# A fused linear-attention and GELU-MLP block: twelve small DMAs moved to ScalarE's queue, and one scaling step moved between two sums

## The chip, the cores and the metric

The kernel runs on one core of one Trainium2 chip. The metric is the device time of one execution in microseconds (us). Three runs of the kernel before gave 207.22, 206.78 and 206.72 us, a median of 206.78 us.

## What is computed

One input x of 2048 tokens by 640 features is normalised once. The result feeds an attention without softmax (32 heads of 20 features) and a two-layer MLP with 1536 hidden features. Both outputs are added to x. All inputs are bf16.

```python
q, k, v = qkv[0], qkv[1], qkv[2]
phi = lambda t: jnp.where(t > 0, t + 1, jnp.exp(t)) + 1e-6
pq, pk = phi(q), phi(k)
kv = jnp.einsum("bhsd,bhse->bhde", pk, v)
z = jnp.einsum("bhsd->bhd", pk)
num = jnp.einsum("bhqd,bhde->bhqe", pq, kv)
den = jnp.einsum("bhqd,bhd->bhq", pq, z)[..., None] + 1e-6
o = num / den
...
return x + _A_ref(xn, A_wqkv, A_wo) + _B_ref(xn, B_w1, B_b1, B_w2, B_b2)
```

The division by `den` is one number for each token and head. The kernel does it on the query side: it multiplies `pq` by 1/den ahead of the last matrix product.

## The kernel before, in words

**Tiles.** The 2048 tokens are 16 tiles of 128, in four chunks of 512 (`NC` = 4, `CW` = 512). The 640 features are five blocks of 128 (`DT` = 5), the 1536 hidden features twelve (`JT` = 12).

**Stages.** Up to about 127 us the kernel normalises x, computes the hidden activations `HG`, the keys, the key-value products, folds these and `wo` into one matrix `Msb`, and computes the transformed queries `PQ` of all chunks (`q_chunk`). The last stage, from 127 us on, is a single long product: for each output block, twelve matmuls of `W2` with `HG` and five of `Msb` with `PQ` are summed in one PSUM bank. For chunks 0, 1 and 2, and for the last feature block of chunk 3, this is done feature-major by `fm` (line 745). For the rest of chunk 3 it is done token by token in `out_piece` (line 710). For chunks 0 to 2 all five twelve-matmul parts of a chunk come first, and then for each block the five `PQ` matmuls and `fm_out`.

**After a sum.** `fm_out(c, nb)` adds bias and residual on VectorE (line 751), and issues a DMA transpose from SyncE's queue (line 755), which brings the block back to token-major. `fm_store(c)` (line 760, SyncE's queue) stores a chunk once its transposes have landed. `x_turn` and `x_turn_last` (lines 674 and 679) are DMA transposes of the residual, also in SyncE's queue.

**Denominators.** Each chunk passes through six steps before its `PQ` may be used in the product:

- `den_parts(c)`: five VectorE instructions (lines 630 and 633) form the products of `PQ` and z.
- `den_gather(c)`: four DMAs of 64 KB (line 644) bring the four partition groups of a head beside each other.
- `den_inv(c)`: a VectorE sum (line 649) and a reciprocal (line 652).
- `den_spread(c)`: four DMAs of 32 KB (line 658) copy the reciprocals to all partitions of a head.
- `rden_scale(c)`: five VectorE multiplications (line 664) scale `PQ` in place. `PQ` block j of the chunk may enter the product after the j-th.

The buffers of these steps (`yv`, `y4`, `rdv`) lie in the tensor that the profile calls `xn_tm`. So a gather is `xn_tm<-xn_tm` and a spread is `xn_tm<-rden`.

**What sets the order.** Each engine executes its instructions in the order in which the Python code records them. A small planner (`Planner.ins`) adds the semaphore waits. There are no due times. VectorE, TensorE, SyncE and ScalarE each have one queue, and an instruction that waits holds up all those recorded after it on the same engine. SyncE's queue, in order, holds from chunk 1 on: half of gather 1, `x_turn(1)`, half of spread 1, the five transposes of `fm_out(0)`, half of gather 2, half of spread 2, the store of chunk 0, `x_turn(2)`, `x_turn_last`, the five transposes of `fm_out(1)`, half of gather 3, half of spread 3, the store of chunk 1, the five transposes of `fm_out(2)`, the store of chunk 2, the last transpose, and the last stores. ScalarE's queue holds the other halves of the gathers and spreads, and no other work after 128.3 us.

PSUM has eight banks, handed out in turn by `take`.

Of the kernel before, what the change touches and what calls it, by code (L numbers as in the profile page):

```python
# [112 lines left out]
def bass_parallel_sum__linear_attn_block__dense_activation_gelu__prompt_kernel(  # L113
# [24 lines left out]
    with contextlib.ExitStack() as es:  # L138
# [59 lines left out]
        def take(n):  # L198
            b = ring[0]
            if n == 2 and b % 2:  # L200
                b += 1
            b %= 8
            ring[0] = (b + n) % 8
            return b

        def bank(b, lo=0, hi=512):
            return ps[:, b * 512 + lo: b * 512 + hi]
# [427 lines left out]
                       reads=[r_z, r_PQ[c][j], r_y[c % 2]], writes=[r_y[c % 2]])  # L635

        def dma_q(c, q):
            return "scalar" if c and q % 2 else "sync"

        def den_gather(c):  # L640
            for q in range(MH):
                dst = y4[c % 2][H * q:H * (q + 1)]
                src = yv[c % 2][:, SW * q:SW * (q + 1)]
                Pl.ins(dma_q(c, q), lambda e, dst=dst, src=src: e.dma_start(dst, src),
                       reads=[r_y[c % 2]], writes=[r_y4[c % 2][q]], dma=True)

        def den_inv(c):
            s = c % 2
            Pl.ins(v, lambda e: e.tensor_reduce(out=den_sb[:, s, :], in_=y4[c % 2].rearrange("p m s -> p s m"),  # L649
                                                axis=mybir.AxisListType.X, op=ALU.add),  # L650
                   reads=r_y4[c % 2], writes=[r_den[s]])
            Pl.ins(v, lambda e: e.reciprocal(rden[:, s, :], den_sb[:, s, :]), reads=[r_den[s]], writes=[r_rden[s]])

        def den_spread(c):
            for q in range(MH):
                dst = rdv[c][:, SW * q:SW * (q + 1)]
                src = rden[H * q:H * (q + 1), c % 2, :].unsqueeze(1).to_broadcast([H, MH, SW])
                Pl.ins(dma_q(c, q), lambda e, dst=dst, src=src: e.dma_start(dst, src),
                       reads=[r_rden[c % 2]], writes=[r_rdb[c][q]], dma=True)

        def rden_scale(c):
            cc = slice(c * CW, (c + 1) * CW)
            for j in range(DT):
                Pl.ins(v, lambda e, j=j: e.tensor_tensor(out=PQ[:, j, cc], in0=PQ[:, j, cc], in1=rdv[c], op=ALU.mult),  # L664
                       reads=r_rdb[c] + [r_PQ[c][j]], writes=[r_PQ[c][j]])
# [6 lines left out]
        def x_turn(c):  # L672
            for t in range(c * CH, (c + 1) * CH):
                Pl.ins("sync", lambda e, t=t: e.dma_start_transpose(xnT[:, :, t * P:(t + 1) * P], x_res[:, t, :]),  # L674
                       reads=[r_xr[c]], writes=[r_xT[t], r_xnT[t]], dma=True)

        def x_turn_last():
            for t in range(NT - CH, NT):
                Pl.ins("sync", lambda e, t=t: e.dma_start_transpose(xnT[:, DT - 1:DT, t * P:(t + 1) * P], x_res[:, t, CW:D]),  # L679
                       reads=[r_xr[NC - 1]], writes=[r_xT[t], r_xnT[t]], dma=True)  # L680
# [51 lines left out]
        def den_parts(c, lo, hi):  # L732
            for j in range(lo, hi):
                den_part(c, j)

        NF = NC - 1

        def fm(c, nb, b, lo, hi):
            cc = slice(c * CW, (c + 1) * CW)
            ns = slice(nb * P, (nb + 1) * P)  # L740
            for i in range(lo, hi):
                l, r = (W2[:, i, ns], HG[:, i, cc]) if i < JT else (Msb[:, i - JT, ns], PQ[:, i - JT, cc])
                rd = ([r_W2] + [r_HG[t][i] for t in range(c * CH, (c + 1) * CH)] if i < JT
                      else [r_M[nb], r_PQ[c][i - JT]])
                Pl.ins("tensor", lambda e, l=l, r=r, i=i: e.matmul(bank(b), l, r, start=(i == 0), stop=(i == JT + DT - 1)),  # L745
                       reads=rd, writes=[B_[b]], mark=(i == hi - 1))

        def fm_out(c, nb, b):
            o = (c % 2) * DT + nb
            cc = slice(c * CW, (c + 1) * CW)  # L750
            Pl.ins(v, lambda e: e.scalar_tensor_tensor(out=oT[o], in0=bank(b), scalar=b2c[:, nb:nb + 1],  # L751
                                                       in1=xnT[:, nb, cc], op0=ALU.add, op1=ALU.add),
                   reads=[B_[b], r_b2c] + r_xT[c * CH:(c + 1) * CH],
                   writes=[r_oT[o]] + (r_GT + [r_KVT] + [r for m in r_MT for r in m] if c == 0 else []))
            Pl.ins("sync", lambda e: e.dma_start_transpose(x_res[:, c * CH:(c + 1) * CH, nb * P:(nb + 1) * P], oT[o]),  # L755
                   reads=[r_oT[o]], writes=[r_omn[c][nb]], dma=True)

        def fm_store(c, lo=0):
            dst = ov[c * CW:(c + 1) * CW, lo:D].rearrange("(t p) d -> p t d", p=P)
            stores.append(Pl.ins("sync", lambda e: e.dma_start(dst, x_res[:, c * CH:(c + 1) * CH, lo:D]),  # L760
                                 reads=r_omn[c], dma=True))
# [7 lines left out]
        for c in range(NF):  # L769
            bs = [take(1) for nb in range(DT)]  # L770
            for nb in range(DT):
                fm(c, nb, bs[nb], 0, JT)
            for nb in range(DT):
                fm(c, nb, bs[nb], JT, JT + DT)
                fm_out(c, nb, bs[nb])
            if c + 2 < NC:
                den_parts(c + 2, 0, DT)
                den_gather(c + 2)
            rden_scale(c + 1)
            if c + 2 < NC:  # L780
                den_inv(c + 2)
                den_spread(c + 2)
            fm_store(c)
            if c == 0:
                x_turn(2)
                x_turn_last()
# [46 lines left out]
```

## Time and profile before

| | us |
|---|---|
| median of three runs | 206.78 |
| lowest and highest | 206.72, 207.22 |
| the profiled execution | 206.52 |
| its span, first to last instruction | 204.7 |
| outside the span (206.52 less 204.7) | 1.8 |
| TensorE busy (matmul) | 200.3 |
| VectorE busy | 122.4 |
| ScalarE busy | 73.6 |
| GpSimd busy | 14.4 |

The granted TensorE clock was 1.000 over the whole span. Busy times are those of one profiled execution. PE is TensorE's matmul, PEld its weight load, DVE is VectorE, ACT is ScalarE. SPq and ACTq are the queues from which SyncE and ScalarE issue DMAs; the time of such a row is that of the issue, not of the transfer. "To landing" is the time from the start of the issue to the arrival of the data. In the timeline, rows that follow each other on one engine are merged, and "x5" is the number of instructions in a row.

### The profile page before, as it was taken

How to read it: one execution, taken by the hardware profiler on the slowest of the kernel's cores; microseconds unless marked ns; L12 is line 12 of the kernel's file. 1: busy time of each engine (PE TensorE's matmuls, PEld its weight loads, DVE VectorE, ACT ScalarE, POOL GpSimd, SP SyncE). 2: the span in 40 equal slices, each digit the busy share in tenths (PEclk: the TensorE clock that was granted, in tenths of full speed). 3: DMA queues.
4: the chain of work that ended last, by engine and by line, in shares of the span. 5: the costliest groups of instructions: out<-in, count | busy, mean ns of one | idle time of the engine just before them, and what ended most of it. 6: DMA issues, size and time to landing. Idle time of an engine off the chain costs nothing.

```text
span 204.7 us, 3181 instructions
## 1 busy us (share of the span) xinstructions
PE 200.3 (98%) x1170; PEld 106.5 (52%) x1170; DVE 122.4 (60%) x246; ACT 73.6 (36%) x144; POOL 14.4 (7%) x43
## 2 busy tenths in 40 slices
PE   7999999999999999999999999999999999997996
PEld 2799884444444444644456565444444444442444
DVE  4679664000007899999278899596983593068123
ACT  3589886666676555112144695000000000000000
POOL 3145434000000000000000000000000000000000
DMA  5966989799901111000389544115551743407553
GB/s 183 349 241 123 131 169 124 214 325 245 327 6 29 26 26 26 3 0 0 64 245 327 105 96 91 29 26 115 115 126 32 205 90 76 94 25 209 75 160 122
DMA packets 52549, 25.45 MB, mean 124 GB/s; under 512 B 38118, under 2 KB 52534, under 8 KB 52534
## 3 DMA queue, kind: packets, MB, share of 16 engines
q1 hardware_dynamic: 50510, 24.39, 49.3%
q10 hardware_dynamic: 2024, 0.86, 1.6%
q8 instruction: 9, 0.15, 0.3%
q14 instruction: 6, 0.05, 0.1%
HBM read 12.72 MB, written 2.62 MB: 75 GB/s over the span
## 4 chain that ended last, share of the span: by engine, by line
PE 83%; SPq 9%; DMA 3%; DVE 2%; issue 1%; ACT 0%; DVEq 0%; ACTq 0%
PE ps L381 24%; PE ps L745 17%; PE ps L584 11%; PE ps L573 8%; PE ps L532 8%; PE ps L710 7%; SPq L755 3%; SPq L674 3%; SPq L679 2%; PE ps L563 2%; PE ps L523 2%; PE ps L413 1%; DMA xPK<-in_A_x_dram 1%; DMA xn_tm<-rden 1%; DMA xn_tm<-xn_tm 1%
## 5 line engine op out<-in xcount | busy, mean ns | idle before, releaser
L381 PE MATMUL ps<-xnT,W 128*128 128x256 bf16 (+2 forms) x375 | 50.4, 297 | 0.0
L385 ACT ACTIVATE HG<-ps,b1c 128x256 bf16<-128x256 f32 (+2 forms) x75 | 37.4, 522 | 13.2 <-PE ps L381 11.3
L745 PE MATMUL ps<-HG,W 128*128 128x512 bf16 x192 | 42.1, 379 | 0.0
L381 PEld LDWEIGHTS ps<-xnT,W 128*128 128x128 bf16 x375 | 32.4, 98 | 17.4
L745 PEld LDWEIGHTS ps<-HG,W 128*128 128x128 bf16 x192 | 18.8, 98 | 22.6
L584 PE MATMUL ps<-xnT,Wqkv 128*128 128x512 bf16 x100 | 22.8, 379 | 0.0
L745 PE MATMUL ps<-PQ,Msb 128*128 128x512 bf16 x80 | 18.4, 380 | 1.1 <-DVE PQ L664 1.1
L532 PE MATMUL ps<-Wqkv,xnT 128*128 128x512 bf16 x80 | 17.9, 379 | 0.0
L573 PE MATMUL ps<-xPK,xn_tm 128*128 128x512 bf16 x80 | 17.4, 379 | 0.0
L337 DVE BATCH_NORM_STATS2 stats<-xPK 128x6 f32<-128x320 bf16 x32 | 13.7, 470 | 5.6 <-DMA xPK<-in_A_x_dram 5.6
L584 PEld LDWEIGHTS ps<-xnT,Wqkv 128*128 128x128 bf16 x100 | 11.3, 118 | 8.7
L507 ACT ACTIVATE xn_tm<-ps 128x512 bf16<-128x512 f32 x20 | 11.9, 597 | 9.5 <-PE ps L584 8.9
L510 DVE SCALAR_TENSOR_TENSOR PQ<-ps,xn_tm 128x512 bf16<-128x512 f32 x20 | 13.8, 692 | 2.1
L507 ACT ACTIVATE ek<-ps 128x512 bf16<-128x512 f32 x20 | 11.8, 597 | 8.4 <-PE ps L532 6.4
L649 DVE TENSOR_REDUCE den_sb<-xn_tm 128x128 f32<-128x512 f32 x4 | 4.1, 1037 | 17.7 <-DMA xn_tm<-xn_tm 17.7
L518 DVE CAST b2c<-out_l 128x5 f32<-128x5 bf16 x1 | 0.2, 172 | 23.4 <-DMA out_l<-b2bc 23.4
L751 DVE SCALAR_TENSOR_TENSOR W<-ps,b2c,xnT 128x512 bf16<-128x512 f32 x16 | 11.5, 737 | 4.3 <-PE ps L745 3.9
L745 PEld LDWEIGHTS ps<-PQ,Msb 128*128 128x128 bf16 x80 | 7.8, 98 | 11.4 <-DVE PQ L664 2.5
L532 PEld LDWEIGHTS ps<-Wqkv,xnT 128*128 128x128 bf16 x80 | 7.8, 98 | 9.4
L573 PEld LDWEIGHTS ps<-xPK,xn_tm 128*128 128x128 bf16 x80 | 7.8, 98 | 9.3
L633 DVE SCALAR_TENSOR_TENSOR xn_tm<-PQ,z_sb,xn_tm 128x512 f32<-128x512 bf16 x16 | 12.0, 750 | 0.4
L510 DVE SCALAR_TENSOR_TENSOR xPK<-ps,ek 128x512 bf16<-128x512 f32 x16 | 11.1, 692 | 1.7
(66 smaller groups left out, 150.5 us busy)
## 6 DMA issues: line engine op xcount, KB each, us to landing
xPK<-in_A_x_dram SPq DMA_DIRECT2D x5, 640.0 KB, 6.7
Wqkv<-in_A_wqkv_dram SPq DMA_DIRECT2D x3, 800.0 KB, 6.6
W<-in_B_w_dram SPq DMA_DIRECT2D x1, 1920.0 KB, 15.1
out_dram<-xPK SPq DMA_DIRECT2D x3, 640.0 KB, 3.6
W<-in_B_w_dram SPq DMA_DIRECT2D x2, 640.0 KB, 7.2
xPK<-in_A_x_dram SPq DMA_DIRECT2D x4, 320.0 KB, 6.5
Wo<-in_A_wo_dram SPq DMA_DIRECT2D x1, 750.0 KB, 11.9
xPK<-in_A_x_dram SPq DMA_DIRECT2D x4, 160.0 KB, 4.5
```

What stands on the lines that cost most here:

```text
L337: Pl.ins(v, lambda e: e.bn_stats(stats[:, s, 6 * h:6 * h + 6], x_in[:, t, h * HW:(h + 1) * HW]), reads=[r_x[t]], writes=[r_stats[s][h]])
L381: Pl.ins("tensor", [(lambda e, k=k: e.matmul(bank(b, 0, w), W1[:, k, jb * P:(jb + 1) * P], xnT[:, k, tok], start=(k == 0), stop=(k == DT - ...
L385: Pl.ins("scalar", lambda e: e.activation(HG[:, jb, tok], bank(b, 0, w), ACT.Gelu_apprx_tanh, bias=b1c[:, jb:jb + 1]), reads=[B_[b], r_b1c ...
L507: Pl.ins("scalar", lambda e: e.activation(et, src, ACT.Exp), reads=[B_[b]], writes=[re])
L510: Pl.ins(v, lambda e: e.scalar_tensor_tensor(out=dst, in0=src, scalar=0.0, in1=et, op0=ALU.max, op1=ALU.add), reads=[B_[b], re], writes=[r ...
L532: Pl.ins("tensor", [(lambda e, k=k, b=b, t=t: e.matmul(bank(b), xnT[:, k, t * P:(t + 1) * P], Wqkv[:, k, D:D + CW], start=(k == 0), stop=( ...
L573: Pl.ins("tensor", lambda e, t=t, b=b, f=f: e.matmul(bank(b), xn_tm[:, t, f * P:(f + 1) * P], PK[:, t, 0:CW], start=(t == 0), stop=(t == N ...
L584: Pl.ins("tensor", [(lambda e, k=k, j=j, b=b: e.matmul(bank(b), Wqkv[:, k, j:D:DT], xnT[:, k, cc], start=(k == 0), stop=(k == DT - 1))) fo ...
L633: Pl.ins(v, lambda e: e.scalar_tensor_tensor(out=yv[c % 2], in0=pq, scalar=z_sb[:, j:j + 1], in1=yv[c % 2], op0=ALU.mult, op1=ALU.add), re ...
L710: return lambda e: e.matmul(bank(b, 0, cs.stop - cs.start), l, r[:, cs], start=(i == 0), stop=(i == JT + DT - 1))
L745: Pl.ins("tensor", lambda e, l=l, r=r, i=i: e.matmul(bank(b), l, r, start=(i == 0), stop=(i == JT + DT - 1)), reads=rd, writes=[B_[b]], ma ...
L751: Pl.ins(v, lambda e: e.scalar_tensor_tensor(out=oT[o], in0=bank(b), scalar=b2c[:, nb:nb + 1], in1=xnT[:, nb, cc], op0=ALU.add, op1=ALU.ad ...
```

## The change

Two edits. First, `dma_q`, which chooses the issuing queue of gathers and spreads: before, chunk 0 used SyncE's queue, and chunks 1 to 3 used ScalarE's for odd parts and SyncE's for even ones. After, chunks 1 to 3 use ScalarE's for all four parts. Second, `rden_scale(3)` is recorded after `fm_out(2, 1)`, where before it came after `fm_out(2, 4)`. The scales of the other chunks stay where they were.

```diff
         def dma_q(c, q):
-            return "scalar" if c and q % 2 else "sync"
+            return "scalar" if c else "sync"
...
             for nb in range(DT):
                 fm(c, nb, bs[nb], JT, JT + DT)
                 fm_out(c, nb, bs[nb])
+                if (c, nb) == (NF - 1, 1):
+                    rden_scale(NF)
             if c + 2 < NC:
                 den_parts(c + 2, 0, DT)
                 den_gather(c + 2)
-            rden_scale(c + 1)
+            if c + 1 < NF:
+                rden_scale(c + 1)
             if c + 2 < NC:
                 den_inv(c + 2)
                 den_spread(c + 2)
```

`NF` is 3. No instruction and no DMA is added or removed.

## The prediction

> **What bounds the kernel now.** I read the busy shares first, then the waits of the last stage, then the chain that ended last, then the timeline around the one wait found. From the page's first part:
>
> ```profile
> PE 200.3 (98%) x1170; PEld 106.5 (52%) x1170; DVE 122.4 (60%) x246; ACT 73.6 (36%) x144; POOL 14.4 (7%) x43
> ```
>
> TensorE is the bound, and the time falls only where TensorE stands still. The table of waits between 176 and 190 us (us in total, times, longest) shows such a place:
>
> ```profile
> PEld ps L745 <- DVE PQ L664: 2.5, 5, 1.6
> PE ps L745 <- DVE PQ L664: 1.1, 1, 1.1
> ```
>
> TensorE waits for line 664, the scaling of PQ. The table for 116 to 205 us has the same two rows with the same sums, so only chunk 3's scaling is late. The chain of waits tells why (start, us, what):
>
> ```profile
> 177.73 0.63 SPq L644
> ...
> 178.41 2.17 DMA xn_tm<-xn_tm
> ...
> 180.77 1.04 DVE den_sb L649
> ...
> 183.50 2.23 DMA xn_tm<-rden
> ...
> 185.91 0.43 DVE PQ L664
> ...
> 186.38 1.73 PE ps L745 x5
> ```
>
> Gather, sum and reciprocal, spread, scale, then the matmul, with no slack between. The timeline of SyncE's and ScalarE's queues shows why the gather came so late:
>
> ```profile
> 168.74 1.34 ACTq L644 DMA_DIRECT2D xn_tm<-xn_tm  x2
> ...
> 171.12 6.51 SPq L755 DMA_TRANSPOSE xPK<-W  x5
> 177.73 1.27 SPq L644 DMA_DIRECT2D xn_tm<-xn_tm  x2
> ```
>
> ScalarE issued its half of gather 3 at 168.74, when `den_parts(3)` had ended. SyncE's half stood behind the transposes and went out at 177.73. What the wait costs is read from the weight loads:
>
> ```profile
> 182.34 2.47 PEld L745 LDWEIGHTS ps<-HG,W 128*128 128x128 bf16 x12
> ...
> 187.73 2.47 PEld L710 LDWEIGHTS ps<-W,HG 128*128 128x128 bf16 x12
> ...
> 190.32 0.96 PEld L710 LDWEIGHTS ps<-Msb,PQ 128*128 128x128 bf16 x5
> 191.40 2.47 PEld L710 LDWEIGHTS ps<-W,HG 128*128 128x128 bf16 x12
> ```
>
> A group of 12+5 matmuls undisturbed takes 191.40 - 187.73 = 3.67 us. The group with the wait took 187.73 - 182.34 = 5.39. The stall is worth **1.72 us**: 1.45 before the first PQ load (186.38 against 182.34 + 2.59) and 0.27 because the five loads then came at the scaling's pace of 0.335 us, not at 0.216.
>
> **What the Trainium skill says.** In "DMA: Bandwidth & Descriptors", section "Issuing engines are not separate DMA queues": DMAs issued from any engine run on the same 16 DMA engines, and issuing from several saves only the sequencer's time. The trace agrees: a gather lands 2.2 us after its issue from SyncE (median), 2.6 from ScalarE. So the new queue makes no transfer faster; it only spares the wait behind SyncE's transposes. In "Perfetto Trace Analysis", section "DMA Instruction — HWDGE (DVE, Sync)": the block that makes the descriptors is locked by one issuer at a time. The trace shows some of that: ScalarE's two gathers began 0.95 us apart (151.03, 151.98) beside transposes, and 0.68 was the distance of its two spreads at 182.82 and 183.50 with none.
>
> **The change part by part.**
>
> *Twelve issues leave SyncE's queue* (two gathers, two spreads, three chunks; 0.60 to 0.79 us each). SyncE only runs earlier by this: `x_turn(1)` can start after spread 0, near 136.1 instead of 139.47; the store of chunk 0 no longer stands behind spread 2's wait at 158.0, so it and `x_turn(2)` move up by about 5 us. On the path to the end this is worth nothing by itself, since SyncE's last transposes and stores are followed by TensorE work until 202.85.
>
> *Twelve issues join ScalarE's queue*, four in a row where there were two. Nothing else is queued there after 128.3 us, so nobody waits behind them but the later ones. The last of four starts three distances after the first: 3 x 0.66 = 2.0 to 3 x 0.95 = 2.9 us for gathers, 2.4 taken, as SyncE transposes beside some of them; 3 x 0.68 = 2.0 to 3 x 0.89 = 2.7 for spreads, 2.2 taken. Landing after the last issue: gather 2.6 (bounds 2.2 and 4.0, the shortest and longest shown), spread 2.25 (1.9 and 2.9).
>
> *Chunk 1.* Gather 1 starts at 137.96 as before, is in at 137.96 + 2.4 + 2.6 = 143.0, and `den_inv(1)` starts at 143.1 instead of 141.43: 1.7 us later (at the late bounds 145.0, 3.6 later). On VectorE `fm_out(0)`, `den_parts(2)` and `rden_scale(1)` stand behind it. The scaling moves from 150.92 to 152.6 (late: 154.5). TensorE loads the first PQ of chunk 1 at 158.60, so this costs nothing: 158.6 less 0.5 for the slower pace leaves 5.5 us of cover, 3.6 at the late bounds. The banks that `fm_out(0)` frees are cover enough too: the first of them is taken again by `fm(1, 3)`, some 36 matmuls of 0.216 us after 145.87, at 153.6.
>
> *Chunk 2.* Gather 2 starts at 151.0 + 1.7 = 152.7, lands at 157.7, `den_inv(2)` ends 2.2 us later (180.58 to 182.82 is that step in the chain) at 159.9. `fm_out(1)` can start only when TensorE has its first sum, at 160.10, so the shift is swallowed. With the late bounds it ends at 163.7, and `fm_out(1)` ends near 167.8 instead of 165.16, 2.7 later. Spread 2 lands near 164.4, ahead of `rden_scale(2)` at 168.62.
>
> *Chunk 3, where the gain is.* All four gathers start at 168.74: landed at 168.74 + 2.4 + 2.6 = 173.7 instead of 180.58. `den_inv(3)` and its waits: + 2.24 = 176.0. Spreads: + 2.2 + 2.25 = 180.4 instead of 185.74. First scaled block: + 0.17 + 0.43 = **181.0** instead of 186.34. TensorE wants the first at 182.34 + 2.59 = 184.93, and to hide the slower pace of the scaling (4 x 0.12) it must be there by 184.5. So 3.5 us of slack, and the stall goes whole. At the early bounds the block is ready at 180.2, at the late ones at 184.0, or 186.7 with chunk 2's 2.7 us on top.
>
> *The scale moved up.* Five instructions of 0.42 us, no DMA. `fm_out(2, 1)` ends near 180.2 (no longer held back by `den_inv(3)` until 182.71), then VectorE waits about 0.3 us for the spread, and `fm_out(2, 2)` to `(2, 4)`, their transposes on SyncE, the last `fm_out` and the adds of the last tiles stand behind that wait. The scale takes until 182.3 (1.76 us for five, as at 185.91), TensorE's last sum of chunk 2 is there at 182.7, so the three end near 184.5 (before: 186.0). Their banks come round again at the very end, near 201, so TensorE doesn't notice. Without the move, in these numbers, the scale would start near 183.5, after the fifth sum, and the first block would be ready near 184.0: just in time too, so I give the move itself nothing.
>
> *What is late next.* No other wait of TensorE is in the tables after 127 us. The end is the last matmul, 0.31 us of VectorE and the last store, all of which move up together. SyncE's tail: transposes of chunk 2 done near 189, store 2 then, the last transpose landed near 192, store 3, the tiles' stores from 192.5; before, they came at 194.30, 194.73, 198.47 and 198.89. VectorE's wait of 4.5 us for an output buffer at 200.99 goes too, and it cost nothing, for TensorE ended the kernel.
>
> **Sum.** The profiled execution's 206.52 - 1.72 = 204.80. The median of the runs is 0.26 above the profiled one: 206.78 - 1.72 = **205.06 us**, 0.8% faster.
>
> **The rivals.**
>
> *A, late but not too late* (9%): distances and landings towards the late bounds, scale ready between 184.5 and 186.3. For: ScalarE's gathers now run beside x_turn and store traffic that comes earlier (DMA share 1.01 at 161 to 164 us before). Against: gathers beside transposes showed 2.4 to 2.7. Half the gain: 205.9.
>
> *B, no gain* (10%): all late bounds at once, 186.7 ready, 0.36 later than now: 207.1; or the stall goes and SyncE's stores set the end, at about the old 206.8. Against: the store of the last piece waits only for VectorE.
>
> *C, slower* (8%): SyncE's transfers, freed of their waits, run into each group of ScalarE's DMAs, and each landing takes the 4.9 us that the slowest transpose took. Then `den_inv(1)` is 4.5 us late, gather 2 lands at 163.3, `den_inv(2)` ends at 165.5, gather 3 starts at 173.2, `den_inv(3)` ends at 183.2, and the first scale is ready at 183.2 + 2.7 + 4.9 + 0.6 = 191.4: 5.1 us later than now, 211.9. It decides from 5.3 us of lateness over my estimate (186.34 - 181.0), and costs one for one. Against: no gather or spread of the trace took over 4.0.
>
> **How the numbers follow.** The forecast has 73%: its own range is 204.6 to 205.5, from the runs' scatter of 0.5 and from small gains at the tail. Rival A spreads to 206.5, which takes in the lower edge of B. Range 204.6 to 206.4, with some 82% in it. About 0.3% (0.62 us) is what a measurement of this kernel can tell from no change. Faster by more: 0.73 and two thirds of A, 0.79. Within: the rest of A and B, 0.13. Slower: 0.08.
>
> **What would show it.** After: no row "ps L745 <- DVE PQ L664" of more than a few tenths; four ACTq rows of line 644 from 168.7 on; line 649 of chunk 3 near 174; line 664 of chunk 3 near 181; the group of 12+5 at 182 us taking 3.67. Chunk 1's line 649 near 143. It is wrong if line 664 of chunk 1 starts after 158, if chunk 3's comes after 184.5, or if the stall goes and the span stays.

## The result, and the profile after

| | before, us | after, us |
|---|---|---|
| median (6 runs each) | 206.75 | 204.95 |
| lowest and highest | 206.47, 207.22 | 204.26, 205.31 |
| the profiled execution | 206.52 | 205.15 |
| its span | 204.7 | 203.5 |

The ratio is 0.9908, with a 95% interval of 0.9888 to 0.9927: 0.9% faster.

The two profiled executions differ by 1.37 us, the medians by 1.80. In the profile after, the last stage (line 745) happens to begin at 128.08 us, in the one before at 127.52, and all that the change touches comes later. So the cleaner measure is the length of the last stage, from the start of the first row of line 745 to the start of the last row of line 710 (the last five matmuls). The two rows of TensorE before (start, us, what):

```profile
127.52 13.11 PE L745 MATMUL ps<-HG,W 128*128 128x512 bf16 x60
...
202.39 0.44 PE L710 MATMUL ps<-Msb,PQ 128*128 128x128 bf16 x5
```

And after, where one matmul record of the first row is missing:

```profile
128.08 13.11 PE L745 MATMUL ps<-HG,W 128*128 128x512 bf16 x59
...
201.22 0.44 PE L710 MATMUL ps<-Msb,PQ 128*128 128x128 bf16 x5
```

The stage took 202.39 - 127.52 = 74.87 us before, and 201.22 - 128.08 = 73.14 after: **1.73 us less**. I use this measure for all kernels below, one profile for each.

First, the table of waits of the kernel after, from 116 to 205 us (us in total, times, longest), in the rows that answer to those of before:

```profile
DVE den_sb L649 <- DMA xn_tm<-xn_tm: 16.1, 4, 6.6
...
DVE PQ L664 <- DMA xn_tm<-rden: 1.6, 1, 1.6
```

The two rows in which TensorE waited for line 664 are gone. In their place VectorE waits 1.6 us for the spread ahead of that line, and nobody waits for VectorE. The weight loads of the kernel after show the same (start, us, what):

```profile
182.90 2.47 PEld L745 LDWEIGHTS ps<-HG,W 128*128 128x128 bf16 x12
185.49 0.96 PEld L745 LDWEIGHTS ps<-PQ,Msb 128*128 128x128 bf16 x5
186.57 2.47 PEld L710 LDWEIGHTS ps<-W,HG 128*128 128x128 bf16 x12
```

The group of 12+5 now takes 186.57 - 182.90 = 3.67 us; it took 5.39. The chain that ended last has no DMA and no scaling in it any more:

```profile
174.48 10.74 PE ps L745 x49
...
186.95 9.06 PE ps L710 x42
...
201.70 0.29 DVE out_l L720
```

It is TensorE from 120 us, where I cut it, to the last piece's sum. Next, chunk 3's steps. The timeline of ScalarE's queue has all four gathers and all four spreads in one row each:

```profile
170.31 2.67 ACTq L644 DMA_DIRECT2D xn_tm<-xn_tm  x4
177.80 2.58 ACTq L658 DMA_DIRECT2D xn_tm<-rden  x4
```

The timeline of VectorE has the sum and the scale that wait for them:

```profile
175.74 1.04 DVE L649 TENSOR_REDUCE den_sb<-xn_tm 128x128 f32<-128x512 f32 x1 [3.78 <-DMA xn_tm<-xn_tm]
...
182.43 1.76 DVE L664 TENSOR_TENSOR PQ<-PQ,xn_tm 128x512 bf16<-128x512 bf16 x5 [1.60 <-DMA xn_tm<-rden]
```

Line 649 comes 5.0 us earlier than before, line 664 3.5 us earlier (5.6 and 4.0, counted from the start of the stage). The first scaled block is ready at 182.43 + 0.43 = 182.86; TensorE wants it at 185.49, less 0.48 for the scaling's slower pace. So 2.2 us of slack are left.

### The profile page after: what moved, and what is told of

It reads as the page before. It is cut to its first block, busy times and chain, and to the rows that moved or that the text cites. A ratio compares the mean times of both kernels' runs of the same rounds, so it can differ in the third digit from the quotient of the medians.

```text
span 203.5 us, 3162 instructions
## 1 busy us (share of the span) xinstructions
PE 199.4 (98%) x1153; PEld 106.7 (52%) x1170; DVE 122.1 (60%) x246; ACT 73.6 (36%) x144; POOL 14.4 (7%) x43
## 4 chain that ended last, share of the span: by engine, by line
PE 90%; DMA 5%; DVE 2%; SPq 1%; issue 1%; POOL 0%; DVEq 0%
PE ps L745 29%; PE ps L381 21%; PE ps L584 11%; PE ps L573 8%; PE ps L532 8%; PE ps L710 7%; DMA xPK<-in_A_x_dram 3%; PE ps L563 2%; PE ps L523 2%; DMA xnT<-xn_tm 1%; DVE stats L337 1%; PE ps L598 1%; PE ps L616 1%; SPq L263 0%; DVE xn_tm L358 0%
## 5 line engine op out<-in xcount | busy, mean ns | idle before, releaser
L745 PE MATMUL ps<-PQ,Msb 128*128 128x512 bf16 x78 | 17.8, 379 | 0.1
```

## The experiments

The question after the result was not whether the stall had gone, but which part of the change removed it. "Stage" is the measure defined above; before it is 74.87, after 73.14. The kernel before, run again beside these kernels, had medians of 206.41 to 206.83. The stage repeats well: in all eight kernels without a stall it is 73.14 or 73.15.

| kernel | median, us | ratio to before, 95% interval | stage, us |
|---|---|---|---|
| queue edit only | 204.77 | 0.9896 to 0.9931 | 73.15 |
| move of the scale only | 206.60 | 0.9969 to 1.0002 | 74.99 |
| only gather 3 leaves SyncE | 204.87 | 0.9900 to 0.9931 | 73.15 |
| all but gather 3 leave SyncE | 204.72 | 0.9892 to 0.9923 | 73.14 |
| only spread 2 leaves SyncE | 204.97 | 0.9902 to 0.9953 | 73.14 |
| SyncE's order only | 204.95 | 0.9888 to 0.9950 | 73.15 |
| after, three copies of delay | 205.00 | 0.9900 to 0.9955 | 73.15 |
| after, seven copies of delay | 205.87 | 0.9957 to 0.9997 | 74.18 |
| after, store of chunk 0 late | 204.71 | 0.9883 to 0.9940 | 73.14 |
| after, store and x_turns late | 205.67 | 0.9932 to 0.9970 | 73.75 |

**The two edits apart.** The first keeps only `dma_q`:

```diff
-            return "scalar" if c and q % 2 else "sync"
+            return "scalar" if c else "sync"
```

> Only the first edit: gathers and spreads of chunks 1 to 3 all in ScalarE's queue, the scale of chunk 3 stays behind fm_out(2, 4). Queue theory (the stall came from the half of gather 3 that stood behind SyncE's transposes): the scale of chunk 3 starts near 184 us, after the fifth sum, and the stall is gone, 205.0 us. Move theory (the scale had to go ahead of the sums): the scale is held by the sums, and half or more of the 1.7 us stays, 206 us or more.

Measured: 204.77 us, stage 73.15. In its timeline the scale waits for the fifth sum and is still in time:

```profile
182.96 0.75 DVE L751 SCALAR_TENSOR_TENSOR W<-ps,b2c,xnT 128x512 bf16<-128x512 f32 x1 [0.33 <-PE ps L745]
183.63 1.75 DVE L664 TENSOR_TENSOR PQ<-PQ,xn_tm 128x512 bf16<-128x512 bf16 x5
```

The second keeps only the moved scale:

```diff
             for nb in range(DT):
                 fm(c, nb, bs[nb], JT, JT + DT)
                 fm_out(c, nb, bs[nb])
+                if (c, nb) == (NF - 1, 1):
+                    rden_scale(NF)
...
-            rden_scale(c + 1)
+            if c + 1 < NF:
+                rden_scale(c + 1)
```

> Only the second edit: the scale of chunk 3 between fm_out(2, 1) and fm_out(2, 2), queues as before. Queue theory: the spread of chunk 3 still lands near 185.7 us, so the stall stays, 206.8 us; up to 1 us more if the three sums that now stand behind the scale make the last transposes and stores late. Move theory: the stall is gone, 205.0 us.

Measured: 206.60 us, an interval that includes 1, and a stage of 74.99, 0.12 longer than before. Its table of waits from 116 to 204 us has the stall back:

```profile
PEld ps L745 <- DVE PQ L664: 2.6, 5, 1.7
DVE PQ L664 <- DMA xn_tm<-rden: 1.8, 1, 1.8
PE ps L745 <- DVE PQ L664: 1.2, 1, 1.2
```

The scale stands earlier in VectorE's queue, and waits there for the same late spread. So the whole gain belongs to the queues, none to the move. The possible loss at the tail, from sums standing behind the scale, was not seen either.

**Which of the twelve DMAs.** In the next three kernels `dma_q` is told whether it serves a gather ("g") or a spread ("s"). First, before with gather 3 alone taken from SyncE:

```diff
-            return "scalar" if c and q % 2 else "sync"
+            return "scalar" if c and (q % 2 or (kind, c) == ("g", 3)) else "sync"
```

> Before with one thing changed: the two even DMAs of gather 3 go to ScalarE's queue. Queue theory: line 649 of chunk 3 starts near 174 us instead of 180.8, the scale near 184, and two moved DMAs bring the whole gain, 205.0 us. If the gain came from relieving SyncE's queue (ten of the twelve issues stay there): no gain, 206.8 us.

Measured: 204.87 us, stage 73.15; line 649 of chunk 3 at 173.93. Two DMAs bring the whole gain. Then the complement, after with gather 3's half back in SyncE's queue:

```diff
-            return "scalar" if c else "sync"
+            return "scalar" if c and (q % 2 or (kind, c) != ("g", 3)) else "sync"
```

> After with one thing undone: the two even DMAs of gather 3 go back to SyncE's queue. Strict queue theory (gather 3 itself must leave SyncE): the stall is back, 206.8 us. Wider theory (SyncE's queue runs earlier once spread 2, for which it waits at 158 us, is gone, so gather 3 would go out near 174 us there too): scale ready near 184.5 to 185, at most 0.3 us of stall, 205.0 to 205.4 us.

Measured: 204.72 us, stage 73.14, the whole gain as well. So my theory in its strict form, that gather 3 had to leave SyncE's queue, **fell**. In this kernel's SyncE queue the half of gather 3 goes out at 173.47, where before it was 177.73:

```profile
153.65 0.41 SPq L760 DMA_DIRECT2D out_dram<-xPK  x1
154.30 6.83 SPq L674 DMA_TRANSPOSE xnT<-xPK  x4
161.38 5.17 SPq L679 DMA_TRANSPOSE xnT<-xPK  x4
...
173.47 1.27 SPq L644 DMA_DIRECT2D xn_tm<-xn_tm  x2
```

The queue ahead of it is some 4 us earlier. These lines of the kernel before say where those 4 us were lost:

```profile
152.74 1.44 SPq L644 DMA_DIRECT2D xn_tm<-xn_tm  x2
158.00 1.25 SPq L658 DMA_DIRECT2D xn_tm<-rden  x2
159.44 0.47 SPq L760 DMA_DIRECT2D out_dram<-xPK  x1
160.15 5.72 SPq L674 DMA_TRANSPOSE xnT<-xPK  x4
```

SyncE had nothing to do from 154.18 to 158.00: its half of spread 2 waited for the reciprocal of chunk 2, with the store and 13 transposes behind it. If that wait is the root, then moving spread 2 alone is enough:

```diff
-            return "scalar" if c and q % 2 else "sync"
+            return "scalar" if c and (q % 2 or (kind, c) == ("s", 2)) else "sync"
```

> Before with one thing changed: the two even DMAs of spread 2 go to ScalarE's queue; both halves of gather 3 are where they were, and the scale is not moved. Root-wait theory (SyncE's queue is late because it waits at 158 us for the reciprocal of chunk 2, with the store of chunk 0 and 13 transposes behind): x_turn(2) starts near 155.5, the even half of gather 3 goes out near 173 to 174, line 649 of chunk 3 starts near 177, the scale near 184, and the whole gain is there, 205.0 us. Count theory (only the number of issues taken out of SyncE's queue matters, 0.6 us each): gather 3 goes out 1.2 us earlier, and about 1.2 of the 1.7 us are gained, 205.6 us.

Measured: 204.97 us, stage 73.14. `x_turn(2)` starts at 155.20, which is 4.95 earlier than before, although the two issues taken out last only 1.25; gather 3's half goes out at 173.34. The last test moves no DMA to another queue and no scale. It only changes SyncE's order, so that SyncE has other work while the reciprocal is made:

```diff
+            if c == 0:
+                fm_store(0)
+                x_turn(2)
             if c + 2 < NC:
                 den_inv(c + 2)
                 den_spread(c + 2)
-            fm_store(c)
             if c == 0:
-                x_turn(2)
                 x_turn_last()
+            else:
+                fm_store(c)
```

> Before with no DMA moved to another queue and no scale moved: only SyncE's own order changes, its half of spread 2 is recorded behind the store of chunk 0 and x_turn(2) instead of ahead of them. Root-wait theory: SyncE does not stand still from 154.2 to 158.0 us any more, the even half of gather 3 goes out near 174 us, line 649 of chunk 3 starts near 177, TensorE's stall before chunk 3's PQ is gone, 205.0 us. If gathers or spreads must leave SyncE's queue: the stall stays, 206.7 us.

Measured: 204.95 us, stage 73.15. In its SyncE queue:

```profile
155.14 6.32 SPq L674 DMA_TRANSPOSE xnT<-xPK  x4
161.51 1.27 SPq L658 DMA_DIRECT2D xn_tm<-rden  x2
163.03 4.96 SPq L679 DMA_TRANSPOSE xnT<-xPK  x4
...
174.65 1.27 SPq L644 DMA_DIRECT2D xn_tm<-xn_tm  x2
```

The count theory, by which only the number of issues taken out matters, falls with this run: the number is the same as before.

**How much slack is left, and what it costs beyond it.** Copies by ScalarE are put ahead of gather 3, three in one kernel and seven in another (shown here); they read the denominators' products and write to a buffer that nobody reads:

```diff
                 den_parts(c + 2, 0, DT)
+                for _ in range(7 if c == 1 else 0):
+                    Pl.ins("scalar", lambda e: e.activation(ek[:, 0, :], yv[1], ACT.Copy),
+                           reads=[r_y[1]], writes=[r_ek[0]])
                 den_gather(c + 2)
```

> After with three ScalarE copies of 512 columns (an estimate of 0.6 us each, from the 0.597 us of line 507) put ahead of gather 3 in ScalarE's queue; their output is used by nobody. Slack theory: the first scaled block of chunk 3 was ready 2.2 us ahead of need in the changed kernel, so 1.8 us of delay cost nothing, 205.0 us. If the chain had no slack: 206.7 us.

> The same with seven copies, an estimate of 4.2 us of delay. Slack theory: 2.0 us over the slack, paid one for one in a wait of TensorE before line 745's first PQ load of chunk 3, 206.9 us. If lateness of this scale were not what the time hangs on: 205.0 us.

Measured: 205.00 us with three, stage 73.15, no stall. This run tests less than I meant: the first gather went out only 1.2 us later than after, counted from the start of the stage (43.42 against 42.23), and the scale's first block was ready only 0.6 later (55.39 against 54.78). So it shows that 0.6 us are free, not 1.8.

With seven 205.87 us, stage 74.18, which is 1.04 more than after. The time was expected a full microsecond higher, and the timeline shows why it is not: here too the delay was smaller than I meant. The first gather went out 3.7 us later than after (45.91 against 42.23), not 4.2, and the scale's first block was ready 3.35 us later (58.13 against 54.78). That is 1.15 over the slack of 2.2, and 1.04 was paid. With the size put right, the price beyond the slack is about one for one. The first PQ weight load of chunk 3 in the kernel with seven copies:

```profile
185.72 0.10 PEld L745 LDWEIGHTS ps<-PQ,Msb 128*128 128x128 bf16 x1 [0.88 <-DVE PQ L664]
```

**What made gather 2 slow.** In the kernel after, gather 2 and line 649 of chunk 2 ran far over my numbers. ScalarE's row of the four gathers, the two SyncE rows beside it, and line 649, all from its timeline:

```profile
153.23 3.20 ACTq L644 DMA_DIRECT2D xn_tm<-xn_tm  x4
154.35 0.41 SPq L760 DMA_DIRECT2D out_dram<-xPK  x1
155.02 6.78 SPq L674 DMA_TRANSPOSE xnT<-xPK  x4
161.51 1.04 DVE L649 TENSOR_REDUCE den_sb<-xn_tm 128x128 f32<-128x512 f32 x1 [6.63 <-DMA xn_tm<-xn_tm]
```

From the first issue to line 649 it took 8.3 us. Two kernels take the company away. The first records the store of chunk 0 behind the x_turns:

```diff
-            fm_store(c)
             if c == 0:
                 x_turn(2)
                 x_turn_last()
+            fm_store(c)
```

> After with the store of chunk 0 recorded behind x_turn(2) and x_turn_last, so that x_turn(2) starts near 153 us and the 640 KB store comes near 164 us. It asks what made gather 2 late in the changed kernel (line 649 of chunk 2 at 161.5, 8.3 us after the gather's first issue, where the prediction had 5.2). Store theory: without the store beside it line 649 starts 5 to 6 us after the gather's first issue, near 158.5. Transpose theory: x_turn(2) beside it does the same harm, 8 us, near 161. The time stays at 205.0 us either way, as chunk 2 has cover.

Measured: line 649 at 159.05, 6.6 us after the first issue at 152.47; 204.71 us, stage 73.14. Neither theory had it right: without the store 1.7 us are won, and 6.6 is still more than the 5.4 of the changed kernel's gather 3. The 1.7 are not the store's alone to explain, since x_turn(2) now starts with the gather (152.27), where in the changed kernel it started 1.8 us behind it. The second takes the x_turns away from gather 2 too, and puts both beside gather 3:

```diff
+            if c == 1:
+                fm_store(0)
+                x_turn(2)
+                x_turn_last()
             if c + 2 < NC:
                 den_parts(c + 2, 0, DT)
                 den_gather(c + 2)
...
-            fm_store(c)
-            if c == 0:
-                x_turn(2)
-                x_turn_last()
+            if c:
+                fm_store(c)
```

> After with the store of chunk 0, x_turn(2) and x_turn_last recorded behind fm_out(1), so that gather 2 has no store and no x_turn beside it, and gather 3 has them. Company theory (a group of four gathers takes 5.2 us from its first issue to line 649 alone, 6.6 beside x_turn, 8.3 beside x_turn and the store): line 649 of chunk 2 starts 5 to 5.5 us after gather 2's first issue; gather 3 takes 7 to 8.5 us, the scale of chunk 3 is ready near 185, TensorE stalls 0 to 1 us, 205.0 to 206.0 us. If the slowness of gather 2 came from four issues in one queue: 8 us again for gather 2, and 5.4 for gather 3, 205.0 us.

Measured: 205.67 us. From the first issue to line 649, gather 2 without that company took 4.3 us, and gather 3 beside the store and x_turn(2) took 7.6. TensorE stalled 0.6 (stage 73.75). ScalarE's queue in that kernel:

```profile
152.29 2.59 ACTq L644 DMA_DIRECT2D xn_tm<-xn_tm  x4
...
169.09 3.06 ACTq L644 DMA_DIRECT2D xn_tm<-xn_tm  x4
178.74 3.02 ACTq L658 DMA_DIRECT2D xn_tm<-rden  x4
```

And line 649 of chunks 2 and 3 and line 664 of chunk 3 in its timeline:

```profile
156.60 1.04 DVE L649 TENSOR_REDUCE den_sb<-xn_tm 128x128 f32<-128x512 f32 x1 [2.66 <-DMA xn_tm<-xn_tm]
...
176.69 1.03 DVE L649 TENSOR_REDUCE den_sb<-xn_tm 128x128 f32<-128x512 f32 x1 [5.95 <-DMA xn_tm<-xn_tm]
...
185.13 1.77 DVE L664 TENSOR_TENSOR PQ<-PQ,xn_tm 128x512 bf16<-128x512 bf16 x5 [4.51 <-DMA xn_tm<-rden]
```

A single gather landed 2.2 us (median) after its issue in the first group and 5.1 in the second. Four issues in one queue are not slow; their company is. Gather 2 was even faster than the company theory's 5 to 5.5.

The stall of 0.6 is not gather 3's alone. Spread 3, with the store of chunk 1 issued beside it at 179.94, took 6.4 us from its first issue to line 664, where the changed kernel took 4.6 (177.80 to 182.43). Without these 1.8 us the block would have been in time. It was ready 2.9 us later than after (57.69 us from the start of the stage against 54.78), and 0.6 of that was paid. The kernel with seven copies says the same: 3.35 later, 1.04 paid. By both, 2.3 us were free.

## Why the prediction was right, point by point

**The size of the stall held.** 1.72 us from the two groups of weight loads; the last stage became 1.73 us shorter and the median fell by 1.80. With TensorE busy through the rest of the stage, what the stall cost was what could be won.

**Chunk 3's chain held in its order, and was late in its times.** I had the first scaled block at 181.0 us. The profile after begins its stage 0.56 later, which makes 181.6; it came at 182.86, 1.3 late, inside my bounds. (The early one is added up wrongly: its terms give 179.7, not 180.2. Nothing hangs on it.) Line 649 at 175.74 against 173.9 + 0.56 is where that comes from, and two terms make it up. Gather 3 was issued 1.0 later than I had it (170.31 against 169.30), and took 5.4 us to line 649 where I had 5.2 (2.4 + 2.6 and 0.2 of waits).

**The step that was mis-sized is chunk 2.** "Gather 2 starts at 152.7, lands at 157.7" was 153.23 and some 161.3 by the profile after: 8.3 us to line 649, where even my late bounds gave 7.0. So `fm_out(1)` was not "swallowed" but began at 163.45, 2.8 later than TensorE had its first sum (160.10 + 0.56), and its five sums, which then followed each other without a wait (3.29 us in all), ended 1.0 us late. This is the 1.0 us by which gather 3 was late. I had taken the longest landing shown before (4.0) as the bound, though I had myself moved x_turn(2) and a 640 KB store onto the gather. The page of the Trainium skill that I cited ("DMA: Bandwidth & Descriptors", "Issuing engines are not separate DMA queues") says that all issuers share the same 16 DMA engines and interleave. The landings fit this: in the kernel with late x_turns a gather took 2.2 us in the median without that company and 5.1 in it, and in the changed kernel the slowest of gather 2 took 6.2. It cost no time, since 2.2 us of slack were left: the 3.5 us of slack that the prediction had counted, not its estimate of the landings, kept the forecast right.

**One step was wrong.** Of the issues leaving SyncE's queue I wrote that this "is worth nothing by itself". The kernels with only spread 2 moved, with all but gather 3 moved, and with SyncE's order alone changed show that it is worth the whole gain by itself. I had seen that the store and x_turn(2) would move up by 5 us, but had not followed the queue to gather 3's half at its end. There are two ways to the same 1.7 us, each enough: gather 3 leaves the queue, or the queue stops standing still at spread 2. The change does both, and they don't add.

**The move of the scale**, which I gave nothing, gave nothing: 73.15 against 73.14 with and without it.

**The rivals.** A, and B in its first form, needed the block ready between 184.5 and 186.7; it was ready at 182.86. B's second form, SyncE's stores setting the end, did not come either: the chain ends in TensorE's matmuls and the last piece's sum. The kernel with late x_turns is rival A made to happen (a stall of 0.6). C needed landings of 4.9 in every group. Gather 2 of the changed kernel had one of 6.2, with a median of 3.2; gather 3 had a median of 3.3, spread 3 of 1.9. Lateness from company is real, then, but only one group of six had a landing over 4.0.

## What to carry to other kernels

Read a DMA queue as you read an engine: an issue that waits for a semaphore holds up everything recorded behind it (here SyncE's queue, from 154.18 to 158.00), and the harm can show 20 us later at a step that has nothing to do with that wait. Before spreading DMAs over more queues, look for the gap in the queue, and for work from behind that can go into it; here the reordering alone was worth as much as twelve moved DMAs. And when a queue is freed, check what its transfers now run beside: a group of small gathers took nearly twice its time beside a large store and transposes (8.3 us against 4.3), and only slack kept that from costing anything.

## What the runs showed of the hardware that was not expected

- Four 64 KB gathers from one queue, with no store and no x_turn beside them: 2.59 us for the four issues, 4.3 us from the first issue to the instruction that reads them. It was 6.6 beside the four transposes of x_turn(2), 7.6 and 8.3 beside these and a 640 KB store.
- I had taken 0.8 us between ScalarE's gathers beside transposes, from a distance of 0.95 before. In the changed kernel gather 3's four issues took 2.67 us beside transposes, 0.68 apart; only in gather 2 was one issue long, 1.23 us where the shortest took 0.61. So transposes beside gather 3 did not stretch its issues, and no run here shows that the lock named in the prediction stretched the one at 0.95.
- The harm goes both ways: x_turn(2)'s four issues took 6.78 us beside gather 2 and the store. They took 5.72 beside the store in the kernel before, and x_turn(1)'s took 5.18 there.
- ScalarE's queue issued the first DMA behind seven copies 3.97 us after the first copy began (169.49 to 173.46), though the copies' row ends 4.60 us after its start. With three copies it was 1.33 us (170.00 to 171.33), and the row ends at 1.95. In both, the issue did not wait for the copy ahead of it to end.
